# One list of sixteen steps in place of a repeated pair: the order of scores, maxima and P times V in a two-block attention kernel

## Chip, cores and metric

The kernel runs on one core of a Trainium2 chip. The metric is the device time of one execution in microseconds (us); the figure compared is the median of several runs. The profile is one execution, recorded by the hardware profiler.

## The reference, cut to what matters

Two attention blocks over 2048 positions with model width 640 and 32 heads of 20 are computed and laid side by side. Block A attends to 8 positions, two apart; block B to all 2048. All is float32.

```
def _B_ref(x, wqkv, wo):
    qkv = (x @ wqkv).reshape(B, S, 3, H, Dh).transpose(2, 0, 3, 1, 4)
    q, k, v = qkv[0], qkv[1], qkv[2]
    scores = jnp.einsum("bhqd,bhkd->bhqk", q, k) * (Dh ** -0.5)
    p = _softmax(scores, axis=-1)
    o = jnp.einsum("bhqk,bhkd->bhqd", p, v)
    return o.transpose(0, 2, 1, 3).reshape(B, S, D) @ wo
a = _A_ref(A_x, A_wqkv, A_wo)      # 8 keys for each query, two positions apart
b = _B_ref(B_x, B_wqkv, B_wo)
return jnp.concatenate([a, b], axis=-1)
```

## The kernel before

The kernel first projects A's and B's inputs (TensorE, called PE), then runs one long loop for B's attention, with A's attention and A's output projection worked in beside it, and at the end projects B's output.

**Units and steps.** B's 32 heads go in 8 groups of four, the queries in 4 blocks of 512, the keys in 16 blocks of 128. A *step* is one block of keys for one group and one block of queries; 16 steps are a *unit* (`NKB` is 16). There are 512 steps (`NS`); the loop in the order described here covers the first 488 of them (`NS - LEAD`), 30 units and half a unit.

**What a step needs.** For each of four heads (two planes `pl` by two row halves `r`) there is a score matmul: keys are stationary, queries move, 62 rows, and the result is one PSUM bank of 128 x 512. ScalarE (ACT) makes its exponential, `e`, and so empties the bank. A *P* (`b_pv`, line 769) multiplies the exponentials of one step by V: four matmuls of 32 columns, side by side. Two P add up in one bank, and ACT copies the sum to `more`; GpSimd (POOL) adds it to `braw`.

**Maxima.** The softmax of a unit needs the maximum of each query's scores before its exponentials are made. They are computed 24 steps ahead (`LEAD`) from a matmul of their own: the same product with queries stationary, 60 rows, one bank for each half `r`. VectorE (DVE) reduces a bank to one column. Both halves in two neighbouring banks can go in one *double* reduction of 128 x 1024 (output `128x2`), or each bank in a *single* one of 128 x 512 (output `128x1`). When the maxima of a unit are complete, `max_rows` (line 634) folds and transposes them on DVE (`mx<-mx`, `mtr<-mx`), splits them in two parts on POOL (`mtr<-mtr`), stores them with four DMAs (`mdr<-mtr`) and loads them back as two rows of the queries (`bq<-mdr`). Two more rows of each score matmul (62 in place of 60) then subtract the maximum from the scores. The first score of the unit waits for this load.

**The names in the rows.** `ps_st` is PSUM, eight banks of 512 columns. `ps_st<-bq,bk` is a score matmul, `ps_st<-bk,bq` one for a maximum, `ps_st<-e,vb` a quarter of a P. `ps_st<-ww,aot` is A's output projection and `ro` the copy of its result, stored by `oa<-ro`. `akv`, `al`, `am`, `ao`, `turn`, `back` and `tr_d` belong to A's attention, which POOL computes; `vb` is V of a group, loaded once for four units. `sm`, `s_d`, `rb` belong to the division by the softmax's sum (`normalize`, line 664). `PEld` rows are weight loads. Every instruction is recorded at line 60, a helper, so rows are told apart by names.

**The order.** `b_pairs` (line 847) writes out the order of PE's work by hand. A *two* (`b_two`, line 808) is a pair of matmuls on the two halves of PE's rows, which run side by side: `ss` is two scores, `MM` two maxima with a double reduction, `sm` a score and a maximum with a single reduction. `P` is a P; `G` is `group()` (line 996): one half of a row block of A's output projection, 15 matmuls, and then all small DVE operations that have been collected in `beside` since the last G (`flush`, line 991). `PAIR` (line 844) serves two steps and is used seven times in a unit; `BESIDE` (line 845), also two steps, is used once, after the eighth P of a unit:

```
PAIR = "P ss MM sm P sm ss MM sm sm".split()
BESIDE = "G ss sm MM sm P P ss sm MM sm".split()
```

A unit has 64 scores and 64 maxima (16 `MM` and 32 `sm`), 16 P and one G. Banks are given out by `one` and `two` (lines 142 and 148), which pick the bank that is free first by the program's own running estimate of each engine's time. Each engine works through its queue in the order written.

**Queues.** `after(n, ...)` puts an action n steps later. SyncE (SP) issues nearly all DMAs, one after the other, and waits in its queue for what the next one needs. Of `max_rows`, POOL's parts come one step after G, the stores three, the load four. A's output tile is turned by five DVE transposes (`a_turn`, line 474), put into `beside` in the step before G. POOL's work for A is added at every fourth step.

Of the kernel before, what the change touches and what calls it, by code (L numbers as in the profile page):

```python
# [40 lines left out]
NKB = 16  # L41
NS = NG * NQC * NKB
LEAD = 24
# [21 lines left out]
def attention_pair(ctx, tc, xa, wqk_a, wv_a, wo_a, xb, wqk_b, wv_b, wo_b, oa, ob):  # L65
# [13 lines left out]
    def after(n, fn, *args):  # L79
        due.setdefault(now[0] + n, []).append((fn, args))  # L80
# [4 lines left out]
    def small(us, op, *args):  # L85

        t = dve.us
        op(*args)
        dve.us = t + us
# [26 lines left out]
    def bank():  # L116

        if read_at:
            n = one(pe.us + 0.2)
            pe.us = max(pe.us + 0.2, read_at[n]) + 2.2  # L120
            behind_v[0] = True
            act.us = max(act.us, pe.us + 0.05)
        else:
            n = free.pop(0)
        t = psb[:, n]
        taken[id(t)] = (n, t)
        return t
# [14 lines left out]
    def one(t, *but):  # L142

        at = [1e9] + read_at + [1e9]
        return min((n for n in range(8) if n not in but), key=lambda n: (
            max(t, read_at[n]), -max(t, at[n]) - max(t, at[n + 2])))
# [48 lines left out]
    def x_pieces(x, n, second=None):  # L195

        t = columns(n)
        src = x[:, n * 512:(n + 1) * 512].rearrange("(k p) c -> p k c", p=128)

        def piece(a, b):  # L200
            u = t[a // (KC - 1)]
            m = a % (KC - 1)
            split(u[:, 0, m:m + b - a], u[:, 1, m:m + b - a], src[:, a:b], "p", second)
        return t, [lambda a=a, b=b: piece(a, b) for a, b in PAIRS]
# [103 lines left out]
    t, more = x_pieces(xa, 1)  # L308
# [6 lines left out]
    for n in (2, 3):  # L315
        t, more = x_pieces(xa, n)
# [125 lines left out]
    done_a = []  # L442
# [191 lines left out]
    def max_rows(m4, m1, q, qc):  # L634

        mt = sb.tile([128, 3, 32], F32R, tag="mtr", bufs=2, name="mtr")
        md = dr.tile([2, GH * 512], F32, tag="mdr", bufs=4, name="mdr")
        raw = mt[:, 0].bitcast(F32)

        def parts():  # L640
            gp.tensor_copy(mt[:, 1], raw)
            gp.tensor_tensor(mt[:, 2], raw, mt[:, 1].bitcast(F32), ALU.subtract)

        def store():
            for b in range(4):
                sp.dma_start(md.rearrange("t (j b c) -> b j t c", b=4, c=32)[b], mt[32 * b:32 * b + 16, 1:].bitcast(F32))

        def load():
            for r in range(2):
                sp.dma_start(q[r * HALF + BS:r * HALF + BM, qc].bitcast(F32),  # L650
                             md[:, r * 1024:(r + 1) * 1024].rearrange("t (p c) -> t p c", p=2))
        def turn():

            small(0.17, dve.tensor_reduce, m1[:, :16], m4.rearrange("p r a c -> p (r a) c"), AX.X, ALU.max)
            small(0.21, dve.transpose, raw, m1)
            after(1, parts)
            after(3, store)
            after(4, load)
        if loop[0] is None:
            after(1, turn)  # L660
        else:
            beside.append((turn,))
# [73 lines left out]
    P = {}  # L736
# [32 lines left out]
    def b_pv(i):  # L769
        u, kb = divmod(i, NKB)  # L770
        g, qc = divmod(u, NQC)
        n, part = divmod(kb, 2)
        if read_at:
            t = max(pe.us + 0.12, exp_at.pop(i))
            if part == 0:
                o = one(t)
                accs[u] = o, psb[:, o]
                t = max(t, read_at[o])
                read_at[o] = 1e9
            pe.us = t + 0.866  # L780
            behind_v[0] = True
        elif part == 0:
            accs[u] = None, bank()
        o, acc = accs[u]
        for j in range(GH):
            pe.matmul(acc[32 * j:32 * j + 32, :], stacks[g][2][:, kb, j * VC:j * VC + 32], P[i][j % 2][:, j // 2],
                      start=(part == 0), stop=(part == 1))
        del P[i]
        if part == 0:
            return  # L790
        del accs[u]
        act.us = max(act.us, pe.us + 0.322)
        if n == 0:
            raws[u] = sb.tile([128, 512], F32, tag="raw", bufs=2, name="braw")
            act.copy(raws[u], acc)
        else:
            more = spare[n % 2][:, n // 2 % 2]
            act.copy(more, acc)
            after(1, pool, raws[u], raws[u], more, ALU.add)
        if o is None:  # L800
            give(acc)
        else:
            read_at[o] = act.us + 0.25
        if kb == NKB - 1:
            last = g == NG - 1
            normalize(raws.pop(u), g, qc * 512, 2 if last else 3, (lambda: out_last(qc)) if last else None)
# [35 lines left out]
                read_at[n] = dve.us + 0.13  # L842

    PAIR = "P ss MM sm P sm ss MM sm sm".split()
    BESIDE = "G ss sm MM sm P P ss sm MM sm".split()

    def b_pairs(pv, group):

        scores = ((i, pl, r) for i in range(NS - LEAD) for pl in range(2) for r in range(2))
        maxima = ((m, j) for m in range(LEAD, NS) for j in range(2))  # L850
        steps = iter(range(-LAG, NS))
        half = []
        for i in range(0, NS - LEAD, 2):
            for t in BESIDE if i % NKB == NKB // 2 else PAIR:
                if t == "P":
                    yield
                    pv(next(steps))
                elif t == "G":
                    group()
                elif t == "ss":  # L860
                    b_two([("s", *next(scores)) for _ in range(2)])
                elif t == "MM":
                    m, j = next(maxima)
                    max_tiles(m)
                    b_two([("m", m, j, r) for r in range(2)])
                    max_end(m, 1)
                else:
                    s = next(scores)
                    shut = bool(half)
                    m, j, r = half.pop() if shut else (*next(maxima), 1 - s[2])  # L870
                    max_tiles(m)
                    if not shut:
                        half.append((m, j, 1 - r))
                    b_two([("s", *s), ("m", m, j, r)])
                    if shut:
                        max_end(m, 1)
# [39 lines left out]
    steps = iter(range(LEAD))  # L916
# [3 lines left out]
    def v_group(n, half, s):  # L920
        p = bank()
        rows15(p, lambda xi, k: chunk(XB[n], xi, k)[:, s % 4 * 128:s % 4 * 128 + 128], WV[half])
        ve = ones[s % 4]
        act.copy(ve[:, :16 * VC].rearrange("p (h c) -> p h c", c=VC)[:, :, :DH],
                 p[:, :320].rearrange("p (h d) -> p h d", d=DH))
        give(p)
        c = 16 * VC + 11 * half
        after(1, sp.dma_start, vb_d[s * 128:(s + 1) * 128, half * 16 * VC:half * 16 * VC + c], ve[:, :c])
# [11 lines left out]
    v_late = V_GROUPS[-LAG:]  # L940
# [55 lines left out]
    def group():  # L996

        for _ in range(2 if now[0] - loop[0] > NS - 60 else 1):
            out_piece()
        flush()  # L1000

    steps = b_pairs(lambda i: b_pv(i) if i >= 0 else v_group(*v_late.pop(0)), group)
    next(steps)
    for i in range(NS + LAG):
        g, sub = divmod(i, NQC * NKB)
        if sub == 4 and g + 1 < NG:
            k_loads, q_loads = b_pieces(g + 1)
            for n, fn in enumerate(k_loads + q_loads + [lambda g=g + 1: v_piece(g, 0, NKB)]):
                after(1 + 2 * n, fn)
        if i in (NS - 56, NS - 40):  # L1010
            out_first((i - NS + 56) // NKB)
        tick()
        if loads and i % 2:
            loads.pop(0)()
        if i > 14 and i % 4 == 3 and next(a_work, 0) == 0:
            for d in done_a:
                d[0] -= 1
        if i % NKB == NKB // 2 - 1 and done_a and done_a[0][0] <= 0:
            beside.append((lambda d=done_a.pop(0): a_turn(*d[1:]),))
        turn_parts()  # L1020
        if i == 1:
            load_out(wo_a, WO, (1,))

            spare += [sb.tile([128, 2, 512], F32, tag="last0", bufs=2, name="more") for _ in range(2)]
        if i < NS - LEAD:
            next(steps, None)
            if not left_a[0] and not WO_b:
                load_out(wo_b, WO_b)
            continue
        read_at.clear()  # L1030
        flush()
        if i < NS:
            b_qk(i)
        if i % 2:
            b_pv(i - LAG - 1)
            b_pv(i - LAG)
            if fill:
                fill.pop(0)()
# [57 lines left out]
```

## Time and profile before

| | |
|---|---|
| Runs | 1796.36, 1791.25, 1795.83 us, median 1795.83 |
| Profiled execution | 1793.7 us, of which the span of instructions is 1791.9 |
| Busy over the span | PE 1776.2, DVE 1340.3, ACT 1325.5, POOL 1222.7 us |
| Granted PE clock | 0.998 |
| The loop | from about 480 to 1690 us of the span |

Busy times are averages over parts with different limits, so the loop is read by itself. PE's busy time includes waits inside matmuls that are pipelined. Rows with a count merge neighbouring operations of the same names, whatever their shapes: a row of 45 reductions named `128x1` holds doubles too. A duration in a group is from the start of an operation to its end, and on DVE and ACT the end of one overlaps the start of the next.

### The profile page before, as it was taken

How to read it: one execution, taken by the hardware profiler on the slowest of the kernel's cores; microseconds unless marked ns; L12 is line 12 of the kernel's file. 1: busy time of each engine (PE TensorE's matmuls, PEld its weight loads, DVE VectorE, ACT ScalarE, POOL GpSimd, SP SyncE). 2: the span in 40 equal slices, each digit the busy share in tenths (PEclk: the TensorE clock that was granted, in tenths of full speed). 3: DMA queues.
4: the chain of work that ended last, by engine and by line, in shares of the span. 5: the costliest groups of instructions: out<-in, count | busy, mean ns of one | idle time of the engine just before them, and what ended most of it. 6: DMA issues, size and time to landing. Idle time of an engine off the chain costs nothing.

```text
span 1791.9 us, 31505 instructions
## 1 busy us (share of the span) xinstructions
PE 1776.2 (99%) x11211; PEld 985.1 (55%) x11211; DVE 1340.3 (75%) x1838; ACT 1325.5 (74%) x2597; POOL 1222.7 (68%) x1072
## 2 busy tenths in 40 slices
PE   9999999989999999999999999999999999999999
PEld 8888888878444444444444444444444444444469
DVE  3100232357999999999999999999999999999400
ACT  4222322222899999999999999999999999988981
POOL 0000058857688988899898988988998988445441
PEclk9999999999999999999999999999999999999999
DMA  6323596876634443454435344443543443212123
GB/s 225 115 94 110 177 309 244 290 225 194 157 104 116 121 127 112 120 145 138 130 98 149 105 116 138 131 121 116 147 124 110 122 125 104 58 43 63 55 70 113
DMA packets 193014, 240.30 MB, mean 134 GB/s; under 512 B 90972, under 2 KB 121308, under 8 KB 191864
## 3 DMA queue, kind: packets, MB, share of 16 engines
q1 hardware_dynamic: 192280, 237.63, 44.5%
q8 instruction: 88, 1.44, 0.3%
q10 hardware_dynamic: 576, 0.66, 0.1%
q14 instruction: 70, 0.57, 0.1%
HBM read 173.29 MB, written 64.91 MB: 133 GB/s over the span
## 4 chain that ended last, share of the span: by engine, by line
PE 87%; ACT 5%; DVE 4%; POOL 1%; DMA 1%; issue 1%; SPq 0%; POOLq 0%; ACTq 0%
PE ps_st L60 87%; ACT e L60 4%; DVE mx L60 4%; ACT more L60 1%; POOL akv L60 1%; DMA bq<-qb_d 1%; DMA stg<-wv_b 1%; POOL braw L60 0%; DMA mdr<-mtr 0%; SPq L60 0%; DVE xl L60 0%; ACT braw L60 0%; POOL ao L60 0%; POOL al L60 0%; DVE pr L60 0%
## 5 line engine op out<-in xcount | busy, mean ns | idle before, releaser
L60 DVE TENSOR_REDUCE mx<-ps_st 128x2 f32<-128x1024 f32 (+1 forms) x1512 | 1209.5, 872 | 61.9 <-PE ps_st L60 61.0
L60 ACT ACTIVATE e<-ps_st 128x512 f32<-128x512 f32 x2048 | 1059.4, 616 | 31.4 <-PE ps_st L60 12.3
L60 PE MATMUL ps_st<-bq,bk 62*128 62x512 f32 x2048 | 636.3, 455 | 2.3 <-DVE mx L60 0.6
L60 PE MATMUL ps_st<-bk,bq 60*128 60x512 f32 x2048 | 578.3, 431 | 4.8 <-DMA bq<-qb_d 3.8
L60 PEld LDWEIGHTS ps_st<-bq,bk 62*128 62x128 f32 x2048 | 276.3, 183 | 535.5 <-ACT e L60 366.1
L60 PE MATMUL ps_st<-e,vb 128*32 128x512 f32 x4096 | 536.7, 603 | 1.1
L60 POOL TENSOR_TENSOR braw<-braw,more 128x512 f32<-128x512 f32 x224 | 287.6, 1284 | 155.0 <-ACT more L60 143.9
L60 POOL TENSOR_TENSOR akv<-akv,aq 128x1280 f32<-128x1280 f32 x64 | 189.0, 2953 | 239.3 <-DVE w L60 236.6
L60 POOL TENSOR_TENSOR akv<-akv 128x640 f32<-128x640 f32 (+3 forms) x304 | 284.1, 935 | 23.8
L60 PEld LDWEIGHTS ps_st<-bk,bq 60*128 60x128 f32 x2048 | 277.0, 185 | 21.5 <-DVE mx L60 11.6
L60 ACT COPY ro<-ps_st 128x480 f32<-128x480 f32 (+1 forms) x124 | 61.2, 496 | 214.8 <-PE ps_st L60 159.7
L60 PEld LDWEIGHTS ps_st<-e,vb 128*32 128x32 f32 x4096 | 85.1, 108 | 160.0 <-issue 82.9
L60 POOL TENSOR_TENSOR akv<-akv,al 128x1280 f32<-128x1280 f32 x64 | 152.0, 2376 | 12.9 <-DMA akv<-va_d 12.8
L60 ACT COPY more<-ps_st 128x512 f32<-128x512 f32 x224 | 132.9, 593 | 20.5 <-PE ps_st L60 19.3
L60 PE MATMUL ps_st<-wc,xn 128*128 128x480 f32 x576 | 136.0, 381 | 0.0
L60 PE MATMUL ps_st<-ww,xn 128*128 128x320 f32 x768 | 127.8, 317 | 1.7 <-DVE ww L60 1.7
L60 PEld LDWEIGHTS ps_st<-ww,xn 128*128 128x128 f32 x768 | 114.8, 190 | 22.5 <-ACT ve L60 8.0
L60 PEld LDWEIGHTS ps_st<-wc,xn 128*128 128x128 f32 x576 | 108.2, 188 | 17.5 <-ACT xn L60 0.2
L60 PE MATMUL ps_st<-xn,w 128*128 128x512 f32 x480 | 115.7, 390 | 0.0
L60 PEld LDWEIGHTS ps_st<-xn,w 128*128 128x128 f32 x480 | 90.1, 188 | 19.3
L60 ACT CAST pr<-ps_st 128x512 fp32r<-128x512 f32 x40 | 23.5, 587 | 100.9 <-PE ps_st L60 100.9
L60 DVE TENSOR_TENSOR pr<-ps_st,pr 128x512 fp32r<-128x512 f32 x40 | 27.7, 692 | 91.1 <-ACT pr L60 91.1
(64 smaller groups left out, 991.0 us busy)
## 6 DMA issues: line engine op xcount, KB each, us to landing
akv<-ka_d SPq DMA_DIRECT2D x128, 320.0 KB
akv<-va_d SPq DMA_DIRECT2D x128, 320.0 KB
kb_d<-pr SPq DMA_DIRECT2D x20, 512.0 KB
qb_d<-pr SPq DMA_DIRECT2D x20, 512.0 KB
bk<-kb_d SPq DMA_DIRECT2D x16, 640.0 KB
bq<-qb_d SPq DMA_DIRECT2D x64, 160.0 KB
rb<-s_d SPq DMA_DIRECT2D x128, 64.0 KB
stg<-xb SPq DMA_DIRECT2D x12, 512.0 KB
```

The costliest lines, as they stand in the source:

```text
L60: return self.tc.keep_in_program_order(op(*a, **k))
```

## The change

`PAIR` and `BESIDE` as the order of a unit are replaced by one list, `UNIT`, for 16 steps, used once for each of the 30 full units. `PAIR` stays for the half unit at the end. The list has 18 `MM`, 28 `sm` and 18 `ss` in place of 16, 32 and 16, and the same number of scores, maxima and P. G stands after the tenth P of a unit, not after the eighth. `SLOT`, worked out from the list, moves the moment at which `a_turn` is put into `beside` by the same two steps. In `max_rows` the stores come two steps after G, not three.

```
-            after(3, store)
+            after(2, store)
             after(4, load)
...
     PAIR = "P ss MM sm P sm ss MM sm sm".split()
-    BESIDE = "G ss sm MM sm P P ss sm MM sm".split()
-
-    def b_pairs(pv, group):
+    UNIT = (
+        "P ss MM sm P sm ss MM sm sm P ss MM sm P sm MM ss sm sm P sm MM ss P sm MM ss sm sm P ss MM sm P "
+        "sm MM ss sm sm P ss MM sm P sm ss MM ss G sm ss MM sm P sm MM ss P sm MM sm ss P sm MM ss P sm "
+        "MM sm ss P MM MM ss P ss MM sm sm").split()
+    SLOT = UNIT[:UNIT.index("G")].count("P") - 1
+
+    def b_units(pv, group):
...
-        for i in range(0, NS - LEAD, 2):
-            for t in BESIDE if i % NKB == NKB // 2 else PAIR:
+        for i in range(0, NS - LEAD, NKB):
+            for t in UNIT if i + NKB <= NS - LEAD else PAIR * (NKB // 4):
...
-        if i % NKB == NKB // 2 - 1 and done_a and done_a[0][0] <= 0:
+        if i % NKB == SLOT and done_a and done_a[0][0] <= 0:
```

On PE, this is what stands behind a G before (`ww,aot` is G, `e,vb` is a P, or two P where eight matmuls are counted):

```order
L60 MATMUL ps_st<-ww,aot 128x320 x15
L60 MATMUL ps_st<-bq,bk 128x512 x3
L60 MATMUL ps_st<-bk,bq 128x512 x3
L60 MATMUL ps_st<-bq,bk 128x512
L60 MATMUL ps_st<-bk,bq 128x512
L60 MATMUL ps_st<-e,vb 32x512 x8
L60 MATMUL ps_st<-bq,bk 128x512 x3
L60 MATMUL ps_st<-bk,bq 128x512 x3
L60 MATMUL ps_st<-bq,bk 128x512
L60 MATMUL ps_st<-bk,bq 128x512
L60 MATMUL ps_st<-e,vb 32x512 x4
```

And this is what stands there in the changed kernel:

```order
L60 MATMUL ps_st<-ww,aot 128x320 x15
L60 MATMUL ps_st<-bq,bk 128x512
L60 MATMUL ps_st<-bk,bq 128x512
L60 MATMUL ps_st<-bq,bk 128x512 x2
L60 MATMUL ps_st<-bk,bq 128x512 x2
L60 MATMUL ps_st<-bq,bk 128x512
L60 MATMUL ps_st<-bk,bq 128x512
L60 MATMUL ps_st<-e,vb 32x512 x4
L60 MATMUL ps_st<-bq,bk 128x512
L60 MATMUL ps_st<-bk,bq 128x512 x3
L60 MATMUL ps_st<-bq,bk 128x512 x2
L60 MATMUL ps_st<-e,vb 32x512 x4
```

Before, four twos and then two P in a row follow G; now four twos and one P, and the next P comes after three more twos.

On SP, the DMAs from the store of G's result to the maxima's load, in a unit with five transposes of A, before:

```order
L60 DMA oa<-ro 128x320
L60 DMA s_d<-sm 128x16
L60 DMA rb<-s_d 32x512 x4
L60 DMA tr_d<-turn 128x640
L60 DMA bk<-kb_d 22x4096
L60 DMA mdr<-mtr 16x2x32 x4
L60 DMA bq<-mdr 2x1024 x2
L60 DMA akv<-va_d 128x640 x2
```

And in the changed kernel:

```order
L60 DMA oa<-ro 128x320
L60 DMA s_d<-sm 128x16
L60 DMA rb<-s_d 32x512 x4
L60 DMA mdr<-mtr 16x2x32 x4
L60 DMA tr_d<-turn 128x640
L60 DMA akv<-va_d 128x640 x2
L60 DMA bq<-qb_d 20x1024
L60 DMA bq<-mdr 2x1024 x2
```

The stores of the maxima moved ahead of the turned tile, and their load moved behind two loads of A's rows and one of the next group's queries. All of it stands two steps later in the unit.

More of the change, by code (lines that the diff above doesn't have):

```diff
@@ L1000, in group @@
         flush()
-    steps = b_pairs(lambda i: b_pv(i) if i >= 0 else v_group(*v_late.pop(0)), group)
+    steps = b_units(lambda i: b_pv(i) if i >= 0 else v_group(*v_late.pop(0)), group)
     next(steps)
```

## The prediction

> **What bounds the kernel now.** I read the table of busy time by stretches first, to see which engine is full in the loop.
>
> ```profile
> core 0: us, PE busy (x) PEld busy (x) DVE busy (x) ACT busy (x) POOL busy (x), PEclk, DMA share, GB/s
> 800.00:900.00 100.00, 99.71 (x680) 41.94 (x680) 98.11 (x135) 94.01 (x187) 90.36 (x80) 1.00 0.45 129
> 900.00:1000.00 100.00, 99.67 (x681) 43.83 (x677) 96.96 (x137) 92.24 (x183) 88.23 (x77) 1.00 0.42 118
> ```
>
> The reader is to see four engines near their limit. VectorE (DVE) is at 97.5%; PE's 99.7% holds waits as well, so it proves nothing. The loop repeats every 16 steps (a unit), so the next view is DVE alone in order of time, over two units (start, duration, operation, count, and in brackets the idle time before it and what ended it).
>
> ```profile
> 790.34 0.34 DVE L60 RECIPROCAL am<-am 128x32 f32<-128x32 f32 x1
> ...
> 792.00 2.38 DVE L60 TENSOR_REDUCE mx<-ps_st 128x1 f32<-128x512 f32 x3
> 794.97 35.41 DVE L60 TENSOR_REDUCE mx<-ps_st 128x1 f32<-128x512 f32 x45 [0.59 <-PE ps_st L60]
> 830.29 0.62 DVE L60 TENSOR_REDUCE am<-al 128x32 f32<-128x256 f32 x1
> ...
> 831.19 0.21 DVE L60 STREAM_TRANSPOSE mtr<-mx 128x32 f32<-128x32 f32 x1
> 831.77 2.42 DVE L60 TENSOR_REDUCE mx<-ps_st 128x1 f32<-128x512 f32 x3 [0.37 <-PE ps_st L60]
> 834.87 16.54 DVE L60 TENSOR_REDUCE mx<-ps_st 128x1 f32<-128x512 f32 x21 [0.68 <-PE ps_st L60]
> 851.58 8.83 DVE L60 TENSOR_REDUCE mx<-ps_st 128x2 f32<-128x1024 f32 x11 [0.17 <-PE ps_st L60]
> ```
>
> The 45 maxima from 794.97 run without a gap: in the repeated pairs DVE is the bound. It idles only just after G (the projection group, with DVE's small operations). The first unit loses 0.59 us, the second 0.37 + 0.68 + 0.17 = 1.22, on average **0.91 us per unit**. The loop has 30 units with a G: 27 us is all that a better order can win back from waits.
>
> **Part 1: 18 double maxima and 28 single ones in place of 16 and 32.**
>
> ```profile
> L60 DVE TENSOR_REDUCE mx<-ps_st 128x1 f32<-128x512 f32 x878 | 565.7, 680 | 26.1 <-PE ps_st L60 26.1
> L60 DVE TENSOR_REDUCE mx<-ps_st 128x2 f32<-128x1024 f32 x439 | 535.7, 1220 | 2.5 <-PE ps_st L60 2.5
> ```
>
> A double is 1.220 - 0.680 = 0.540 us longer than a single. Means overlap, so I take the true pace from the gapless stretch: 45 operations (30 single, 15 double) from 794.97 to 830.29 are 35.32 us; 45s + 15 x 0.540 = 35.32 gives s = 0.605, and 1.145 for a double. A unit's maxima are now 32 x 0.605 + 16 x 1.145 = 37.68 and become 28 x 0.605 + 18 x 1.145 = 37.55: **0.13 us saved per unit**. The other DVE work is unchanged.
>
> The Trainium skill's "Perfetto Trace Analysis" (section Optimizing Scalar/DVE Operations) gives a DVE operation on PSUM about 125 ns of overhead, so grouping pays on a saturated engine. By that figure two fewer operations would save an estimated 0.25 us per unit; the rows above give 0.065 us per operation, half of it, and the sum goes by the rows.
>
> **Part 2: the two P together after G go.** Here is PE around that G, then DVE and ACT:
>
> ```profile
> 908.56 2.21 PEld L60 LDWEIGHTS ps_st<-ww,aot 128*128 128x128 f32 x15 [0.28 <-ACT e L60]
> 910.96 0.73 PE L60 MATMUL ps_st<-bq,bk 62*128 62x512 f32 x3
> 912.21 1.92 PE L60 MATMUL ps_st<-e,vb 128*32 128x512 f32 x16
> 914.06 0.36 PEld L60 LDWEIGHTS ps_st<-bq,bk 62*128 62x128 f32 x3 [0.84 <-ACT e L60]
> 914.40 0.62 PE L60 MATMUL ps_st<-bk,bq 60*128 60x512 f32 x3
> 914.86 10.64 DVE L60 TENSOR_REDUCE mx<-ps_st 128x1 f32<-128x512 f32 x13 [0.68 <-PE ps_st L60]
> 915.39 1.06 PE L60 MATMUL ps_st<-e,vb 128*32 128x512 f32 x8
> 916.39 0.50 PE L60 MATMUL ps_st<-bq,bk 62*128 62x512 f32 x2
> 917.08 0.39 PE L60 MATMUL ps_st<-bq,bk 62*128 62x512 f32 x1
> 917.39 1.07 PE L60 MATMUL ps_st<-e,vb 128*32 128x512 f32 x8
> ```
>
> One P holds PE for 1.00 us (915.39 to 916.39), two for 1.85 (912.21 to 914.06). The first two (a pair of matmuls) after a P or G takes 0.34 (914.06 to 914.40), later ones about 0.25: 910.96 to 912.21 is 1.25 for four, which leaves 0.16 before the P; elsewhere it is 0.31 (917.08 to 917.39), and I take 0.31. A maximum starts 0.46 after its matmul (914.40 to 914.86); I take 0.50. Time 0 is where PE leaves G (910.96).
>
> Old order, "ss sm MM sm P P ss sm": maxima are ready at 0.84 and last 2.36, so until 3.2; the first sm behind the two P starts at 3.34 and is ready at 3.84. DVE idles 0.64; the row says 0.68, so this arithmetic can be trusted.
>
> New order, "sm ss MM sm P": DVE starts at 0.50 and has work until 2.86; P ends at 2.15, the next sm is ready at 2.65, 0.20 early. Going on through "sm MM ss P sm MM sm ss P sm MM ss P sm MM sm ss P MM MM ss P ss MM sm sm P": each P with three twos costs PE 1.90 and gives DVE 1.75 (MM MM ss: 2.29), with four 2.15 and 2.36. The first maximum behind each P comes 0.06, 0.26, 0.11, 0.31, 0.37, 0.57 us before DVE runs dry. So the **0.68, the 0.59 and the 0.17 go**, but with thin margins, and no bank wait is in them.
>
> **Part 3: G itself.** Before it now stands "P sm ss MM ss" in place of "sm sm". With full banks DVE still holds one double and part of a single (1.1 to 1.7 us) and ACT up to four exponentials; then come small operations, 1.1 us in the second kind of unit, 1.7 in the first. G to the first maximum takes 908.56 to 910.96 plus 0.50, 2.9 us, and sm now comes first, where ss did. Idle: 0 to 0.7 in the second kind (0.37 now), 0 in the first; I take 0.20 and 0, mean 0.10, and allow 0.15 for the thin margins.
>
> **Other engines.** ACT waits too:
>
> ```profile
> 831.08 0.43 ACT L60 COPY ro<-ps_st 128x320 f32<-128x320 f32 x1 [1.09 <-PE ps_st L60]
> 834.26 0.59 ACT L60 COPY more<-ps_st 128x512 f32<-128x512 f32 x1 [0.63 <-PE ps_st L60]
> ```
>
> That is 1.72 us per unit that it can give up before it becomes the bound. The new order should leave it about 0.6 at "P MM MM ss". POOL is busy 89.3% of 40.0 us, 35.7 us per unit, and meets its own cast of the maxima two steps later, behind one more addition of 1.3 us; it still fits 39.2. PE's own work is 16 x 1.00 + 64 x 0.25 + 16 x 0.15 (the slower first two and the 0.31 of each P) + 2.7 for G = 37.1.
>
> **Part 4: the maxima's DMAs.** G moves two steps later and the scores that read the stored maxima don't.
>
> ```profile
> 911.52 0.34 SPq L60 DMA_DIRECT2D oa<-ro  x1
> 911.96 0.38 SPq L60 DMA_DIRECT2D s_d<-sm  x1
> 913.48 1.72 SPq L60 DMA_DIRECT2D rb<-s_d  x4
> 915.30 1.77 SPq L60 DMA_DIRECT2D mdr<-mtr  x4
> 920.24 0.53 SPq L60 DMA_DIRECT2D bq<-mdr  x2
> ```
>
> ```profile
> akv<-va_d SPq DMA_DIRECT2D x128, 320.0 KB
> vb<-vb_d SPq DMA_DIRECT2D x7, 760.0 KB
> ```
>
> From PE's leaving G, the load is issued at 9.3 us, after the stores have landed. The walk above puts the first score that needs it at 14.3 (now two P and eight twos, 4.7 us, later). A small transfer lands 1.5 us after its issue (911.96 to 913.48), so by 11.3. What now stands between, 0.6 to 1.0 MB of akv and other loads (1.8 MB with vb in 7 units), is issued inside the stores' landing time. It is hidden if it moves at 302 GB/s, as here:
>
> ```profile
> 885.00:886.00 1.00, 1.00 (x10) 0.16 (x8) 1.00 (x2) 1.00 (x3) 0.84 (x4) 1.00 1.11 302
> ```
>
> 1.0 MB takes 3.5 us from 6.1 on: cost 0.
>
> **Sum.** Per unit 0.91 - 0.25 + 0.13 = 0.79 us; by 30 units 23.7. The profiled execution is 1793.7 (span 1791.9), so 1770.0. The median of the runs is 2.1 above that execution, hence **1772**. What lies before and after the loop is unchanged but for a G two steps later.
>
> **Rivals.**
> *Banks.* Eight PSUM banks serve ACT, DVE and P. The walk has PE never waiting for one, yet "P MM MM ss" wants four for maxima beside P's own and those that ACT still reads. If PE waits 0.1 us more than the margin behind each of the six P, 0.6 us comes back: 0.2 saved per unit, 6 us, 1790 on the runs' scale. For it: PE, ACT and DVE would all be at 95% or more. Against: the old pairs keep DVE gapless with ACT at about 4.65 of each 4.70. I give 1778 to 1798.
>
> *The load comes late.* If the load of the maxima waits out what was issued before it, at the mean rate,
>
> ```profile
> DMA packets 193014, 240.30 MB, mean 134 GB/s; under 512 B 90972, under 2 KB 121308, under 8 KB 191864
> ```
>
> 1.0 MB takes 7.5 us from 6.1: it lands at 15.1 with its own 1.5, 0.2 past what DVE's margin of 0.57 covers; with vb 5.7 us more, 5.9 past, in 7 units. Lost: 23 x 0.2 + 7 x 5.9 = 46 us against 23.7 won: 1818. It decides from a landing later than 14.3 + 0.57 + 0.79 = 15.7 on. Against: the short stretches move 302 GB/s. For:
>
> ```profile
> 803.67 3.87 SPq L60 DMA_DIRECT2D back<-tr_d  x4
> ...
> 881.77 0.43 SPq L60 DMA_DIRECT2D vb<-vb_d  x1
> 882.24 6.32 SPq L60 DMA_DIRECT2D back<-tr_d  x4
> ```
>
> Four loads behind vb needed 6.32 us to be issued (3.87 without vb).
>
> The Trainium skill's "DMA: Bandwidth & Descriptors" (section Queues, rings and completion order) says that each DMA engine takes descriptors in ring order; that speaks for this rival, and these last rows agree, though they cannot tell the engines' order from SP's queue.
>
> That the order isn't what the change says is no rival: PE's rows above show it moved.
>
> **How the numbers follow.** The forecast, 1762 (all waits gone, 1.04 us x 30) to 1778: 0.58. Banks: 0.24, of which 0.07 within 0.3% of the old time (about what a measurement of this kernel can tell from no change). The late load, 1801 to 1830: 0.18. Faster 0.75, same 0.07, slower 0.18. The range takes in the first two: 1761 to 1798.
>
> **What would show it.** DVE's view: the 0.68 and 0.59 behind G gone, one wait of 0.2 or less at G, a unit of 39.2 us instead of 40.0. Wrong if new gaps of 0.1 to 0.3 stand behind the six P after G (banks), or PE waits at a unit's first scores for bq<-mdr (the late load), or ACT's waits vanish while DVE's grow.

## The result and the profile after

| | before | after |
|---|---|---|
| Median of the runs (6 each) | 1796.07 us | 1785.88 us (1784.66 to 1786.11) |
| Ratio | 1 | 0.9951, 95% interval 0.994 to 0.9962 |
| Profiled execution | 1793.7 us, span 1791.9 | 1786.11 us, span 1784.3 |
| Granted PE clock | 0.998 | 0.997 |

The changed kernel is faster by 10.2 us. The forecast was 24 us (1772), more than twice as much; the range (1761 to 1798) holds the result.

The busy time by stretches hardly moved: DVE went from 98.11 and 96.96 us of 100 to 98.17 and 97.68. So little can be read from shares; the order of DVE's operations says more. This is DVE alone in order of time, after (start, duration, operation, count, and the idle time before it):

```profile
794.64 37.69 DVE L60 TENSOR_REDUCE mx<-ps_st 128x1 f32<-128x512 f32 x46 [0.24 <-PE ps_st L60]
832.24 0.62 DVE L60 TENSOR_REDUCE am<-al 128x32 f32<-128x256 f32 x1
...
833.14 0.21 DVE L60 STREAM_TRANSPOSE mtr<-mx 128x32 f32<-128x32 f32 x1
834.17 37.87 DVE L60 TENSOR_REDUCE mx<-ps_st 128x1 f32<-128x512 f32 x46 [0.82 <-PE ps_st L60]
871.95 0.34 DVE L60 RECIPROCAL am<-am 128x32 f32<-128x32 f32 x1
...
872.65 1.04 DVE L60 STREAM_TRANSPOSE turn<-ao 128x128 f32<-128x128 f32 x5
873.95 15.32 DVE L60 TENSOR_REDUCE mx<-ps_st 128x1 f32<-128x512 f32 x18 [0.25 <-PE ps_st L60]
889.59 22.43 DVE L60 TENSOR_REDUCE mx<-ps_st 128x2 f32<-128x1024 f32 x28 [0.33 <-PE ps_st L60]
```

In most units all 46 maxima are now one run; the breaks of 0.59 and 0.68 three maxima behind G are gone. Some units still break after the 18th maximum, as at 889.59. Most of what is left stands at G itself: 0.82 us in units whose small operations are `am<-al` and the like (1.11 us, 832.24 to 833.35), 0.25 us in units with five transposes (1.74 us, 871.95 to 873.69). These two units last 39.53 (794.64 to 834.17) and 39.78 us (to 873.95), on average 39.66.

Some units are longer, so the account goes by 20 of them. From one `am<-al` to another they last 794.76 us (594.27 to 1389.03), 39.74 a unit; before, 800.47 us (590.19 to 1390.66), 40.02. A unit is 0.28 us shorter, where 0.79 was forecast. DVE's two kinds of maxima from 600 to 1400 us, before and then after (the number behind the second bar is the idle time ahead of them, gaps of every length counted):

```profile
L60 DVE TENSOR_REDUCE mx<-ps_st 128x1 f32<-128x512 f32 x640 | 412.2, 680 | 16.6 <-PE ps_st L60 16.6
L60 DVE TENSOR_REDUCE mx<-ps_st 128x2 f32<-128x1024 f32 x321 | 391.7, 1220 | 2.0 <-PE ps_st L60 1.9
```

```profile
L60 DVE TENSOR_REDUCE mx<-ps_st 128x2 f32<-128x1024 f32 x364 | 439.8, 1217 | 3.2 <-PE ps_st L60 2.1
L60 DVE TENSOR_REDUCE mx<-ps_st 128x1 f32<-128x512 f32 x564 | 364.5, 681 | 12.1 <-PE ps_st L60 10.7
```

Idle time fell from 18.6 to 15.3 us, in 20 units 0.16 us a unit. That leaves 0.12 of the 0.28 for DVE's work. In 30 units this is 8.4 us; one long unit near the start of the loop loses 1.03 of it (the load, below), and the spans differ by 7.6. The list of waits, which leaves out the shortest gaps, has 18.5 us in 40 places before and 12.8 in 27 after: 0.1 us of the idle time was in gaps too short for the list before, and 2.5 us is now.

The backlog that DVE holds when G starts is the first thing to check. This is the changed kernel in order of time, PE's weight loads of G and DVE's last maximum ahead of them:

```profile
831.11 1.22 DVE L60 TENSOR_REDUCE mx<-ps_st 128x2 f32<-128x1024 f32 x1
831.20 2.20 PEld L60 LDWEIGHTS ps_st<-ww,aot 128*128 128x128 f32 x15 [0.32 <-ACT e L60]
...
870.98 2.20 PEld L60 LDWEIGHTS ps_st<-ww,aot 128*128 128x128 f32 x15 [0.38 <-issue]
```

G starts at 831.20 and the maxima end at 832.24: 1.04 us of work, one double just begun. At the other G it is 870.98 to 871.95, 0.97 us. G's start to the first maximum behind it is 2.97 us both times. 1.04 and 1.11 cover 2.15 of that, so 0.82 is left; 0.97 and 1.74 cover 2.71, so 0.26 is left. The rows say 0.82 and 0.25. Before, the G at 908.56 met more: DVE's maxima lasted until this row, 1.73 us.

```profile
910.29 0.62 DVE L60 TENSOR_REDUCE am<-al 128x32 f32<-128x256 f32 x1
```

ACT's waits for PE in the same stretch (600 to 1400 us) hardly moved in sum, 42.3 us before and 40.6 after. The wait for `ro` fell from 22.5 to 12.6 and that for `more` (12.6) went, but the exponentials now wait 28.0 us in 91 places, where it was 7.2 in 40.

PE behind the G at 831.20, after:

```profile
836.70 1.07 PE L60 MATMUL ps_st<-e,vb 128*32 128x512 f32 x8
838.50 0.61 PE L60 MATMUL ps_st<-bq,bk 62*128 62x512 f32 x2
839.04 1.07 PE L60 MATMUL ps_st<-e,vb 128*32 128x512 f32 x8
```

A P with three twos takes 1.9 us, as the walk had it; one with four takes 2.34 (836.70 to 839.04), where the walk had 2.15. The last two before the next P lasts 0.61 us in place of 0.40, and the weight load of that P lists 0.37 us of waiting for DVE's `mx`: PE does wait for a bank there. No wait of DVE is listed at that place.

### The profile page after: what moved, and what is told of

It reads as the page before. It is cut to its first block, busy times and chain, and to the rows that moved or that the text cites. A ratio compares the mean times of both kernels' runs of the same rounds, so it can differ in the third digit from the quotient of the medians.

```text
span 1784.3 us, 31398 instructions
## 1 busy us (share of the span) xinstructions
PE 1768.5 (99%) x11211; PEld 987.5 (55%) x11211; DVE 1334.4 (75%) x1778; ACT 1325.7 (74%) x2597; POOL 1221.4 (68%) x1072
## 4 chain that ended last, share of the span: by engine, by line
PE 92%; DMA 3%; ACT 2%; DVE 1%; issue 1%; POOL 0%; SPq 0%; ACTq 0%; DVEq 0%; POOLq 0%
PE ps_st L60 92%; DVE mx L60 1%; ACT e L60 1%; DMA bq<-mdr 1%; DMA stg<-wv_b 1%; DMA bq<-qb_d 1%; ACT more L60 1%; DMA bk<-kb_d 0%; POOL akv L60 0%; DMA stg<-xa 0%; SPq L60 0%; ACT al L60 0%; POOL braw L60 0%; DVE xl L60 0%; DVE pr L60 0%
## 5 line engine op out<-in xcount | busy, mean ns | idle before, releaser
L60 PE MATMUL ps_st<-bq,bk 62*128 62x512 f32 x2048 | 617.0, 445 | 2.6 <-DMA bq<-mdr 1.4
L60 PEld LDWEIGHTS ps_st<-bq,bk 62*128 62x128 f32 x2048 | 284.2, 184 | 494.0 <-ACT e L60 369.3
L60 PE MATMUL ps_st<-bk,bq 60*128 60x512 f32 x2048 | 553.1, 435 | 4.0 <-DMA bq<-qb_d 2.4
L60 PE MATMUL ps_st<-e,vb 128*32 128x512 f32 x4096 | 542.9, 604 | 0.2
L60 PEld LDWEIGHTS ps_st<-bk,bq 60*128 60x128 f32 x2048 | 258.0, 185 | 55.4 <-ACT e L60 24.5
L60 POOL TENSOR_TENSOR akv<-akv,al 128x1280 f32<-128x1280 f32 x64 | 152.1, 2377 | 13.7 <-DMA akv<-va_d 13.5
```

Source lines behind the costliest of these rows:

```text
L60: return self.tc.keep_in_program_order(op(*a, **k))
```

## Experiments

Each ratio is to the kernel before, timed beside it on the same chip; its median there was 1794.01 (e1 to e4), 1795.19 (e5 to e8), 1793.44 (e9 to e12) and 1793.82 us (e13 to e16). Times of two groups are therefore comparable to 2 or 3 us only. Lines that merely keep the program's running estimate of an engine's time in step are left out of the edits.

### How much G costs in each order: e5 and e6

```
-                rows15(p, lambda xi, k: ot[:, xi, k], W[half])
+                for k in range(KC):
+                    pe.matmul(p[:, :320], ot[:, 0, k], W[half][0][:, k], start=(k == 0), stop=(k == KC - 1))
```

> The changed kernel with 5 matmuls in each G in place of 15 (A's output projection keeps one of its three passes; the other two are left out), 1.6 us of PE less per unit, everything else as it is. Theory A (DVE is the bound, and what G costs is the time for which DVE finds nothing to do at G): DVE's waits at G, 0.82 and 0.25, go and nothing else changes: 0.5 to 0.6 us per unit, 1768 to 1771. Theory B (PE itself is the bound through the unit, and DVE's waits are only where it shows): most of 1.6 us per unit, 48 us, is won: 1738 to 1750. Theory C (the engines wait for each other by way of the banks, and a wait that goes comes back): under 5 us, 1781 or more.

> The kernel before with the same edit: 5 matmuls in each G in place of 15 (two of the three passes of A's output projection are left out). Theory A: its waits behind G, 0.91 us per unit, go: 27 us, 1768, the same time as the changed kernel with a short G, since the lists then differ by the two doubles alone. Theory B: 48 us, 1747. Theory C: under 5 us.

e5 (the changed kernel): 1770.7 us, ratio 0.9865 (0.985 to 0.9879), 15.2 below the changed kernel. e6 (the kernel before): 1770.6 us, 0.9866 (0.985 to 0.9883), 24.6 below its own base. DVE in order of time, in e5 and then in e6:

```profile
710.34 37.66 DVE L60 TENSOR_REDUCE mx<-ps_st 128x1 f32<-128x512 f32 x46
747.91 0.62 DVE L60 TENSOR_REDUCE am<-al 128x32 f32<-128x256 f32 x1
...
788.99 37.66 DVE L60 TENSOR_REDUCE mx<-ps_st 128x1 f32<-128x512 f32 x46
```

```profile
707.71 37.61 DVE L60 TENSOR_REDUCE mx<-ps_st 128x1 f32<-128x512 f32 x48
...
749.26 16.54 DVE L60 TENSOR_REDUCE mx<-ps_st 128x1 f32<-128x512 f32 x21 [0.63 <-PE ps_st L60]
...
786.36 37.61 DVE L60 TENSOR_REDUCE mx<-ps_st 128x1 f32<-128x512 f32 x48
```

Neither has a listed wait ahead of the first maximum behind G. Two units last 78.65 us in both (710.34 to 788.99, 707.71 to 786.36), 39.33 a unit: 0.33 less than in the changed kernel and 0.68 less than before. That is 10 us and 20 us in 30 units, so e5's total is that of theory A, but not its 0.5 to 0.6 us a unit. The other 5 us of each lie mostly in the last two units of the loop, where a G is twice as long (DVE waits 3.63 and 3.56 us there in the changed kernel, 0.70 and 0.63 in e5).

With a short G both orders take the same time: **the 10 us by which the changed kernel is faster exist only with the long G**. Shortening it is worth 25 us before and 15 after. This does not make the orders alike. The old one still waits 0.63 us behind its two P in every second unit (749.26); the new one waits 0.19 and 0.15 us in the same kind of unit, and its 46 maxima take 37.57 us (710.34 to 747.91) without a listed wait, no less than the 48 of e6, so its two more doubles win nothing in this pair.

### Other orders around G: e1, e2, e16

e1 leaves the old order and only parts the two P:

```
-    BESIDE = "G ss sm MM sm P P ss sm MM sm".split()
+    BESIDE = "G ss sm MM sm P sm MM P sm ss".split()
```

> The kernel before with one edit: the pair with G becomes "G ss sm MM sm P sm MM P sm ss", so its two P no longer stand together; everything in front of G, the 16 double maxima and the stores stay. Theory (the wait at G is set by the DVE work that stands in banks when PE enters G, the 0.68, 0.59 and 0.17 by the two P): those three go, G keeps its 0.37 and 0, so 0.73 us per unit, 30 units: 22 us less than before, 1774, and so faster than the changed kernel. Rival (three engines above 95%: waits only move): what is won behind the P comes back at G or at later P, at most 10 us less, 1786 or more.

1807.0 us, ratio 1.0069 (1.0057 to 1.0081): slower, a miss. DVE in order of time:

```profile
755.87 4.75 DVE L60 TENSOR_REDUCE mx<-ps_st 128x1 f32<-128x512 f32 x6 [0.36 <-PE ps_st L60]
761.66 14.19 DVE L60 TENSOR_REDUCE mx<-ps_st 128x2 f32<-128x1024 f32 x18 [1.05 <-PE ps_st L60]
```

The wait behind the P has moved from the third maximum behind G to the sixth and grown from 0.68 to 1.05. Three P now stand close together ("P sm MM P sm ss P"). The walk of the prediction, carried on over these, has the next maximum ready 6.29 us after PE leaves G and DVE dry at 5.55: it would have told most of this. Two twos between the two P are not enough; the new list puts three or four between any two P behind G.

e2 gives DVE one more maximum directly ahead of the new G:

```
-"... P sm ss MM ss G sm ss MM sm P ..."
+"... P ss MM ss sm G sm ss MM sm P ..."
```

> The changed kernel with the four twos in front of G in another order: "ss MM ss sm G" in place of "sm ss MM ss G". Theory: DVE then has a single maximum more (0.605 us) standing in a bank when PE enters G; its wait at G falls from 0.82 to about 0.2 in the units with A's maximum and from 0.25 to 0 in the others: 0.43 us per unit, 13 us less than the changed kernel, 1773. Rival (waits only move): DVE runs dry between the P and the later first maximum, by about 0.3 to 0.6 us, and the time stays within 3 us of the changed kernel, 1783 to 1789.

1785.82 us, ratio 0.9958 (0.9945 to 0.997): the time of the changed kernel. DVE in order of time, and then DVE and PE at the last two maxima ahead of a G:

```profile
751.46 38.01 DVE L60 TENSOR_REDUCE mx<-ps_st 128x1 f32<-128x512 f32 x46 [0.67 <-PE ps_st L60]
...
791.22 37.85 DVE L60 TENSOR_REDUCE mx<-ps_st 128x1 f32<-128x512 f32 x46
```

```profile
826.51 0.68 DVE L60 TENSOR_REDUCE mx<-ps_st 128x1 f32<-128x512 f32 x1
826.80 0.40 PE L60 MATMUL ps_st<-bk,bq 60*128 60x512 f32 x2
827.24 1.23 DVE L60 TENSOR_REDUCE mx<-ps_st 128x2 f32<-128x1024 f32 x1
827.79 2.47 PE L60 MATMUL ps_st<-ww,aot 128*128 128x320 f32 x15
828.98 0.62 DVE L60 TENSOR_REDUCE am<-al 128x32 f32<-128x256 f32 x1
```

Two things are to be seen. The maximum of 0.6 us added only 0.15 to the backlog at G: 1.19 us (827.79 to 828.98) for 1.04. And the waits at G shrank from 0.82 and 0.25 to 0.67 and one too short to be listed, while the runs of 46 grew from 37.60 and 37.78 to 37.76 (791.22 to 828.98) and 37.92 (751.46 to 789.38). The second fence shows where: the double starts 0.73 us after the single before it (826.51 to 827.24), which needs 0.60 (e10, below), since its matmuls (826.80) now stand behind two scores. What is won at G is lost just ahead of it. PE does not notice: all 16 P of a unit stand at the same distance from G in e2 and in the changed kernel, within 0.02 us. So a listed wait on DVE is not the whole of what an order loses, and not a price either.

e16 puts two twos into the middle of G (nine matmuls, "sm ss", six matmuls and the copy):

```
-G sm ss MM sm P
+G sm ss H MM sm P          # G: k in 0..2; H: k in 3..4, then the copy
```

> The changed kernel with G in two parts: nine of its 15 matmuls, then one score with a maximum and two scores, then the other six matmuls and the copy; nothing is left out, TensorE does the same work. Theory (VectorE runs dry because nothing reaches it for 2.97 us, and TensorE has time to give over the unit): the first maximum comes some 0.9 us sooner, before VectorE has run dry, and most of the 0.53 us per unit goes: 1770 to 1778. Rival (TensorE's work itself is what lacks behind G, so a wait only moves to another maximum): within 3 us of 1785.9.

1806.17 us, ratio 1.0064 (1.0047 to 1.008): 20 us slower than the changed kernel, a miss on the other side of both theories. DVE in order of time:

```profile
756.91 0.69 DVE L60 TENSOR_REDUCE mx<-ps_st 128x1 f32<-128x512 f32 x1
758.63 29.24 DVE L60 TENSOR_REDUCE mx<-ps_st 128x2 f32<-128x1024 f32 x35 [1.03 <-PE ps_st L60]
```

The first maximum does come before DVE is dry (756.91, no wait), but the second then waits 1.03 us for the rest of G. And the next P stands 3.94 us behind G's start (754.81 to 758.75) where it stood 3.58 behind (831.20 to 834.78). The 0.36 us is not made up later: times 30 it is 11 us of the 20. In every second unit three P further on are 0.23 us late as well (2.14 us from one P to the next in place of 1.90); 0.7 us in 15 units is 10 us, about the rest. Why they are late is not shown.

### The load of the maxima: e3

```
-            after(4, load)
+            after(3, load)
```

> The changed kernel with the load of the maxima three steps after G in place of four, ahead of A's rows and of V on SP. If the late load costs what the trace shows at the first scores of some units (DVE waits of 1.03, 0.33, 0.85 and 0.30 us, 2.5 us in all), these waits go: 1 to 3 us less than the changed kernel, 1783 to 1785. If they come from something else, the time stays at 1786 and the waits stay in the trace. If SP's waiting for the stores delays A's rows, POOL waits for them and the time rises by some us.

1786.27 us, 0.9956 (0.9944 to 0.9968): no change. But the edit did not do what was meant. SP and PE in order of time, in the changed kernel and then in e3:

```profile
1041.35 0.41 SPq L60 DMA_DIRECT2D vb<-vb_d  x1
1041.92 2.64 SPq L60 DMA_DIRECT2D bq<-mdr  x2
...
1048.19 0.68 PE L60 MATMUL ps_st<-bq,bk 62*128 62x512 f32 x2 [0.67 <-DMA bq<-mdr]
```

```profile
1039.59 0.40 SPq L60 DMA_DIRECT2D vb<-vb_d  x1
1040.16 2.62 SPq L60 DMA_DIRECT2D bq<-mdr  x2
...
1046.42 0.68 PE L60 MATMUL ps_st<-bq,bk 62*128 62x512 f32 x2 [0.52 <-DMA bq<-mdr]
```

In e3 the load still stands behind A's rows and `vb`; the order of SP's DMAs is the same as in the changed kernel in all 30 units with a G. The waits of the expectation are still there, too: DVE waits 0.88, 0.69, 0.65 and 0.28 us, and PE 1.5 us in all for `bq<-mdr`. So e3 is a second measurement of the changed kernel, and what an earlier load would win is not tested.

In the changed kernel the load is late in a few units, all of them with the load of `vb`. The issue of `bq<-mdr` takes 2.64 us behind `vb` (0.54 in a unit without it), and PE waits 0.67 us. Over the whole kernel PE waits 1.4 us for it, in two places. The Trainium skill's "DMA: Bandwidth & Descriptors" (section Queues, rings and completion order) has descriptors taken in ring order; the longer issue fits this, though a row of SP cannot tell the order of the DMA engines from SP's own queue. The price is 1.4 us and not the 46 of that rival.

### What a double is worth: e4 and e10

e4 undoes the two extra doubles of the list ("MM ss" becomes "sm sm", twice). e10 leaves PE's order as it is and reduces each double as two singles:

```
-                    dve.tensor_reduce(m4[:, :, pq, 2 * ch + j], psb[:, ns[0]:ns[0] + 2], AX.X, ALU.max)
+                    for h in range(2):
+                        dve.tensor_reduce(m4[:, h, pq, 2 * ch + j:2 * ch + j + 1], psb[:, ns[h]], AX.X, ALU.max)
```

> The changed kernel with 16 double and 32 single maxima again: in the second and third pair of the unit one MM and one ss each become two sm, and G's surroundings stay. If a double saves what the gapless stretches show (0.05 to 0.065 us for each operation saved, 0.10 to 0.13 us per unit), 3 to 4 us more than the changed kernel, 1789 to 1790. If the doubles also hold two banks longer and cost waits, no difference or a gain, 1783 to 1787.

> The changed kernel with every double maximum made as two single ones, the same matmuls in the same order in the same banks: 18 operations more per unit, at 0.065 us each 1.2 us more DVE work per unit. If DVE is the bound: 35 us more, 1821. If ACT is, and DVE has slack: nothing or under 10 us more, 1784 to 1796; the two doubles that the change added are then worth nothing by themselves.

e4: 1794.47 us, 0.9999 (0.9991 to 1.0008), 8.6 above the changed kernel, twice what was expected. It is no clean price, since the list's banks fall otherwise and some P come 0.2 us later. e10: 1799.54 us, 1.003 (1.0022 to 1.0039), 13.7 above, 0.46 us a unit: between the two theories. DVE in e10, in order of time:

```profile
716.60 38.44 DVE L60 TENSOR_REDUCE mx<-ps_st 128x1 f32<-128x512 f32 x64
...
756.75 38.38 DVE L60 TENSOR_REDUCE mx<-ps_st 128x1 f32<-128x512 f32 x64 [0.68 <-PE ps_st L60]
```

The 64 maxima of a unit, 0.60 us each, take 0.75 and 0.51 us more than the 46 of the changed kernel (37.69 and 37.87), not 1.2: some of the added work fills gaps that were too short to be listed. And the listed waits fall from 12.8 to 6.8 us in 20 units, 0.3 us a unit. So most of the missing price went into time in which DVE had waited; e10 does not show that DVE had slack in its runs. By the 125 ns per operation of the Trainium skill's "Perfetto Trace Analysis" (section Optimizing Scalar/DVE Operations) 18 operations would have been an estimated 2.25 us a unit; the rows show 0.6, and two singles at 0.60 each against a double at 1.145 make 0.05 us an operation.

### Who sets the pace of the repeated pairs: e7, e8, e9, e12, e11, e13 to e15

e7 takes work off DVE, e8 puts work on ACT, e9 and e12 put one or two of ACT's copies per unit on DVE, e11 takes work off PE:

```
e7:  psb[:, n]  ->  psb[:, n, :480]            (both kinds of maxima)
e8:  +            for _ in range(2):           (before each copy to more or braw)
     +                act.copy(idle_out, idle_in)
e9:  act.copy(more, acc)  ->  dve.tensor_copy(more, acc) for n == 1     (e12: n in (1, 2))
e11: pe.matmul(acc[32 * j:32 * j + 32, :480], ..., P[i][j % 2][:, j // 2, :480], ...)
```

> The changed kernel with the maxima taken over 480 of 512 columns (the last 32 keys of each block are left out of the maximum): 0.033 us less DVE work for each half, 2.1 us per unit, nothing else changes. If DVE is the bound in the pairs (theory A): 64 us less, 1722. If PE's own work is (theory B): nothing or a few us. If the pace of the pairs comes from the three engines' handing banks to each other (theory C): something between, 15 to 45 us less.

> The changed kernel with two small copies (128x64, from and to tiles that nothing else uses) added on ACT behind every second P, about 0.16 us each, 2.6 us of ACT per unit. If ACT has slack in the pairs, as its total of 37 to 38 us of 39.6 says (theory A or B): under 15 us more, below 1800. If ACT's gapless run of eight exponentials and a copy in 4.71 us means that it is a bound like DVE: up to 78 us more, 1850 to 1865. Theory C: between, 1800 to 1840.

> The changed kernel with one of the seven copies to more in each unit (that of the second pair of P) made by DVE in place of ACT: 0.48 us less on ACT, 0.6 us more on DVE, per unit. If ACT with its hand-over to PE sets the pace of the pairs and DVE has slack, as the kernel with shorter maxima and the one with more copies suggest: 0.3 to 0.48 us less per unit, 9 to 14 us, 1772 to 1777, faster than both kernels. If DVE is the bound after all: up to 18 us more, 1800 to 1804. If a copy on DVE only moves a wait: 1783 to 1789.

> The same for two of the seven copies in each unit. If ACT is the bound: twice the gain of one, 18 to 28 us, 1758 to 1768, unless DVE with 1.2 us more per unit (about 39 of 39 us) now becomes the bound, when it is no better than one copy. If DVE is the bound already: 36 us more, 1822.

> The changed kernel with P over 480 of 512 queries (the last 32 of each block are left out): PE has about 0.055 us less for each P, 0.9 us per unit. If PE's own work sets the time everywhere: 26 us less, 1760. If PE sets it only behind G, where it never waits (six or seven P): 0.35 us per unit, 10 us less, 1776. If ACT sets it everywhere: under 3 us, 1783 or more.

| run | us | ratio (95%) | against 1785.9 |
|---|---|---|---|
| e7, DVE 2.1 us a unit lighter | 1788.05 | 0.9963 (0.9948 to 0.9977) | +2.2 |
| e8, ACT 3.5 us a unit heavier | 1861.46 | 1.037 (1.0354 to 1.0385) | +75.6 |
| e9, one copy a unit to DVE | 1803.69 | 1.0054 (1.0041 to 1.0068) | +17.8 |
| e12, two copies a unit to DVE | 1818.43 | 1.0139 (1.0125 to 1.0153) | +32.6 |
| e11, P 0.9 us a unit shorter | 1772.89 | 0.9879 (0.9865 to 0.9892) | -13.0 |

e8's two copies take 0.44 us a pair in the trace, 3.5 us a unit and not the 2.6 expected. e9 and e12 came out as expected for a DVE that is the bound, e8 as for an ACT that is.

e7 was the surprise: 60 us less of DVE's work gained nothing, as if PE alone set the pace. By the list of waits from 600 to 1400 us DVE now waits 44.4 us in 149 places where it waited 12.8 in 27; most of the time that was taken off has turned into waits. ACT in the repeated pairs of the changed kernel shows why DVE is not alone:

```profile
856.11 4.25 ACT L60 ACTIVATE e<-ps_st 128x512 f32<-128x512 f32 x8
860.35 0.59 ACT L60 COPY more<-ps_st 128x512 f32<-128x512 f32 x1
860.83 4.25 ACT L60 ACTIVATE e<-ps_st 128x512 f32<-128x512 f32 x8
```

A pair of steps is eight exponentials and a copy, 4.72 us (856.11 to 860.83), and ACT has no listed wait in it, just as DVE has none. Each of e8, e9 and e12 costs most of what it adds: 2.5 of 3.5, 0.59 of 0.6 and 1.09 of 1.2 us a unit. But e11 gains 0.43 of its 0.9 us a unit with the work of DVE and ACT unchanged, between the two theories for PE: PE's own time counts in a part of the unit, too. The last three runs put a tie of DVE and ACT to the test with columns left out on one side, the other, and both:

```
e14: e11 and  act.activation(P[i][pl][:, r, :480], p[:, :480], AF.Exp, scale=SCALE)
e15: e11 and the maxima of e7
e13: all three
```

> The changed kernel with all three engines of the loop lighter: P times V, the exponentials and the maxima each over 480 of 512 columns (the last 32 columns of each block are left out of the sums, of the exponentials and of the maxima). By rows already taken: the maxima fall from 681 to 651 ns (single) and from 1217 to 1153 ns (double), some 2 us per unit of 16 steps on VectorE; a copy of 512 columns takes 587 ns and one of 320 columns 427 ns on ScalarE, 0.83 ns a column, so 64 exponentials lose 1.7 us per unit; P loses 0.9 on TensorE. Theory (VectorE and ScalarE tied at 4.7 us a pair): only this one of the three kernels gains much, the smaller of the two, 1.4 to 1.7 us per unit against P at 480 alone (1772.9): 42 to 50 us, so 1723 to 1733. Rival 1 (ScalarE alone holds the pace): the same here. Rival 2 (the hand-over between engines, or TensorE, holds the pace): within 8 us of 1773.

> The changed kernel with P times V and the exponentials over 480 of 512 columns (the last 32 queries of each block are left out of both), the maxima whole: ScalarE is 1.7 us per unit lighter, VectorE is not. Theory (tied engines): VectorE still holds the pace, so no more than the 0.1 us a pair that separates them, 1764 to 1774 against 1772.9 with P at 480 alone. Rival 1 (ScalarE alone holds it): the same time as the kernel with all three lighter, 1723 to 1733. Rival 2 (the hand-over): 1773.

> The changed kernel with P times V and the maxima over 480 of 512 columns (the last 32 queries of each block are left out of the sums, the last 32 columns out of each maximum), the exponentials whole: VectorE is 2 us per unit lighter, ScalarE is not. Theory (tied engines): ScalarE still holds the pace, 1764 to 1774 against 1772.9 with P at 480 alone. A rival by which VectorE alone holds the pace once P is shorter: 60 us less, 1713.

e14, ACT lighter: 1777.36 us, 0.9906 (0.9891 to 0.992). e15, DVE lighter: 1776.81 us, 0.9902 (0.9885 to 0.9918). e13, both lighter: 1760.78 us, 0.9814 (0.9799 to 0.9829). Against e11 (1772.89, 0.9865 to 0.9892) neither alone gains; that both lose 4 us is hardly beyond the intervals. Together they gain 12. Their waits for PE from 600 to 1400 us:

| run | ACT's exponentials | DVE's maxima |
|---|---|---|
| changed kernel | 28.0 us, 91 times | 12.8 us, 27 times |
| e11, P shorter | 26.8 us, 75 times | 14.0 us, 24 times |
| e14, ACT lighter too | 52.0 us, 142 times | 9.4 us, 16 times |
| e15, DVE lighter too | 20.9 us, 31 times | 40.3 us, 124 times |
| e13, both lighter too | 31.1 us, 78 times | 28.1 us, 83 times |

The engine that was made lighter waits, the other doesn't: ACT alone or DVE alone as the bound is out, and **of these two both must be made lighter before anything is won**. How far they are tied is another matter. e13 gained 12 us, a little more than the 8 that the rival (hand-over, or PE) allowed and far from the 42 to 50 of the tie, so the tie holds for these 12 us and then a third limit takes over. In e13 both wait for PE, and PE's weight loads wait for their banks in turn (98.8 us for DVE's, 241.4 for ACT's by the list of waits). Whether the third limit is PE's own work, the hand-over of banks or this list's fixed choice of them stays open.

## Where the prediction held and where it failed

**DVE as the bound of the pairs.** Half right. DVE has no listed gap there, and work added to it costs time (e9, e12). But the reading took a gapless row as proof of the one bound. ACT is gapless in the same rows, and e7, e14, e15 and e13 show that taking work off DVE alone wins nothing.

**Part 1, the doubles.** Right in size as far as the account shows it: 0.12 us a unit is left for DVE's work, where 0.13 was taken. The pair with a short G does not show it.

**Part 2, the waits behind the P.** Right in the main. The 0.68, the 0.59 and mostly the 0.17 are gone; listed waits away from G are some 0.1 us a unit. Its sentence that no bank wait is in the P was wrong: a P with four twos takes 2.3 and not 2.15. The first of these takes more than the next margin of 0.11, and gaps too short to be listed come to 0.12 us a unit (2.5 in 20). Together that is a little more than the 0.15 that was allowed.

**Part 3, G itself. This is the step that failed.** It took 1.1 to 1.7 us of backlog on DVE, and of the idle times that followed (0 to 0.7 and 0) it took 0.20 and 0. Measured are backlogs of 1.04 and 0.97 us, below its range, and waits of 0.82 and 0.25, above it: 0.53 on average in place of 0.10. That is 0.43 of the 0.51 us a unit by which the forecast was wrong (0.79 against 0.28), 13 us in 30 units; by the medians it was 14 us too low. The backlog of 1.7 that the trace of before shows at a G belonged to the old order. In the new one, "P sm ss MM ss" ahead of G gives ACT five exponentials and DVE only the last double, and that double has just begun when G starts (831.11 and 831.20). e5 shows what the waits at G are worth: without them a unit is 0.33 us shorter, not 0.53, since waits open elsewhere (5.3 us in 20 units by the list). e2 shows that they are no price by themselves: 0.15 less at G won nothing.

**Other engines.** Nothing in these runs points to POOL. ACT was said to have 1.72 us a unit to give up and to be left about 0.6; its listed waits stay at 2 us a unit, only elsewhere. That is not slack in the pairs.

**Part 4, the load.** Nearly right: PE waits 1.4 us in all, in two units with `vb`, where the cost was put at 0. e3 did not move the load and says nothing on it.

**The rivals.** Banks: the gain came out in its range (1778 to 1798), but not for the reason given. It asked for gaps of 0.1 to 0.3 us behind six P, 0.6 us a unit; hardly any is listed, and the shorter ones come to 0.12. Most of the wait is at G. The late load is real and tiny.

That the result lies in the range is therefore partly luck: the range was drawn for the banks, and the wait at G filled it.

Not settled: what sets PE's pace between one P and the next behind G. In e2 the P stand at the same distances as in the changed kernel, which speaks for PE and its banks and not for DVE's backlog, and e16 agrees (0.36 us more of PE behind G is lost for good). No run takes the banks away by itself.

## What to carry to other kernels

A gapless engine is not yet the only bound: look for a second engine that is gapless in the same rows, since then taking work off the one gained nothing here, and adding to either cost most of it where it met no gaps. When a long block of one engine must be covered, read the others' backlog at its start from what stands directly ahead of it in the new order, and not from the old order's rows: here even the low end of a range read from the old order was too high. To price an obstacle, shorten it in both orders: the differences say what each order loses by it. And look in the trace whether an edit moved what it was meant to move before its time is read as an answer.

## What was not expected of the hardware

- An engine made 5% lighter can leave the time unchanged: e7 took 60 us off DVE, and its interval (0.9948 to 0.9977) overlaps that of the changed kernel (0.994 to 0.9962).
- Splitting one accumulation of 15 matmuls in nine and six, with two twos between that have to be done anyway, put the next P 0.36 us further behind G's start (3.94 in place of 3.58 us).
- Gaps too short for the list of waits count: the same 46 reductions took 37.57 (e5), 37.60 and 37.78 (after), 37.76 and 37.92 us (e2) in rows that show no wait inside.
